# First product of tiles 3 to 8 by seven block products for pairs of tiles, weights streamed from DRAM, in an attention and feed-forward kernel

## The chip, the cores and the metric

The kernel runs on one core of one Trainium2 chip. The metric is the device time of one execution in microseconds: lower is better. TensorE (PE) multiplies, VectorE (DVE), ScalarE (ACT) and GpSimd (POOL) do the elementwise work, and SyncE (SP) issues the DMAs.

## The reference

Windowed attention over 8 batches x 8 heads x 576 positions x 64, then a feed-forward layer with a PReLU between its two products, all in float32:

```python
scores = scale * np.matmul(q, k.transpose(0, 1, 3, 2))
mask_plain = (rel >= 0) & (rel < 32)
mask_dil = (rel >= 0) & (rel < 32 * 4) & (rel % 4 == 0)
...
attn = softmax(where(mask, scores, -1e9))        # heads 0-3 plain, 4-7 dilated
x = (attn @ v).transpose(0, 2, 1, 3).reshape(8 * 576, 512)
h = x @ w_in                                     # 4608 x 512 x 2048
g = np.maximum(h, 0.0) + alpha * np.minimum(h, 0.0)
return g @ w_out                                 # 4608 x 2048 x 512
```

## The kernel before, in words

The 4608 tokens are cut into 9 tiles of 512 (`NTILE`, `TT`), the 2048 hidden columns into 16 slices of 128 (`NF`), the 512 model columns into 4 of 128 (`NC`). Everything is held transposed, so tokens are the free dimension. To keep float32 precision, every operand of the large products is held as a rounded high part and a remaining low part, and a product is three passes (high x high, high x low, low x high: `PASSES`). The weights come in as the 64-bit words of the inputs, are turned into high and low (`Conversion`), and then stay in SBUF, in tags `w0_*` to `w3_*`: `w_in` high and low, `w_out` high and low, each in three spans of slices (0 to 7, 8 and 9, 10 to 15).

A slice `(t, f)` of the feed-forward layer is `ffn_h` (12 matmuls of 128x128 on 128x512: 4 column blocks x 3 passes, into one PSUM bank), then on VectorE `ffn_parts` (PReLU in two operations), on ScalarE `ffn_high` and on VectorE `ffn_low` (the high and low part of g), then `ffn_y` (12 matmuls, 4 banks that collect over all 16 slices of the tile). After the last slice of a tile `ffn_y` copies the banks out and stores them.

Attention goes by 32 pairs of heads, four to a batch (`Pair`, index 4 b + c). For a pair, `load_qk` and `load_v` fetch, `scores` are 72 small matmuls, `maxima` 12 VectorE operations, `exponentials` 10 on ScalarE, `divisions` four on VectorE, `transposes` 5 on TensorE, `copies` 2 on ScalarE, `values` 72 small matmuls; `highs` (ScalarE) and `lows` (VectorE) write x, the input of the feed-forward layer, as high and low parts. A batch has 576 tokens and a tile 512, so a tile waits for the pairs of one or two batches.

The order on TensorE, VectorE, ScalarE and SP is the order in which the program is written (`manual_schedule`); the framework adds the semaphores. First come pairs 0 to 3 alone with the conversion of weights; then a loop over `slices`: tile 0's first 8 slices (`CUT`), tile 1, tile 0's rest (its half sum waits in DRAM, `part`), then tiles 2 to 8. In the loop, iteration n issues `ffn_h` of slice n + 1, `ffn_y` of slice n - 1, and the steps of the pairs that `score_at`, `divide_at`, `turn_at` and `value_at` put there: every second slice until tile 2 begins, then every fourth. Large matmuls are at line 337 (h) and 383 (y), scores at 158, transposes at 214, values at 232.

Of the kernel before, what the change touches and what calls it, by code (L numbers as in the profile page):

```python
# [29 lines left out]
NF = DFF // P  # L30
NROOM = 3
NG = 4
# [19 lines left out]
def tile_window_attention_prelu_ffn(  # L52
# [14 lines left out]
    const = ctx.enter_context(tc.tile_pool(name="const", bufs=1))  # L67
    xp = ctx.enter_context(tc.tile_pool(name="xp", bufs=NROOM))
# [3 lines left out]
    psp = ctx.enter_context(tc.tile_pool(name="psp", bufs=4, space=PS))  # L72
    dram = ctx.enter_context(tc.tile_pool(name="dram", bufs=1, space=bass.MemoryType.DRAM))

    ctx.enter_context(tc.manual_schedule(engines={nc.tensor.engine, nc.vector.engine, nc.scalar.engine, nc.sync.engine}))

# [3 lines left out]
    al = const.tile([P, NF], F32, name="al")  # L80
    nal = const.tile([P, NF], F32, name="nal")
    pr0 = const.tile([P, NR, BK], F32, name="pr0")
# [4 lines left out]
    part = dram.tile([NC, P, TT], F32, name="part")  # L87


# [25 lines left out]

    cells = {}

    def cell(t):
        if t not in cells:
            cells[t] = xp.tile([P, NC, 2, TT], F32R, tag="x", name=f"x_{t}")  # L120
        return cells[t]

# [3 lines left out]
    class Pair:  # L126
# [36 lines left out]
        def scores(self):  # L163
            self.ps = [psp.tile([P, NG + 2, BK], F32, tag=self.banks, name=f"s_{self.id}_{e}") for e in range(2)]
# [43 lines left out]
        def transposes(self):  # L208

            self.tp = [psp.tile([P, 3 - e, P], F32, tag=self.tbanks, name=f"t_{self.id}_{e}") for e in range(2)]  # L210
# [13 lines left out]
        def values(self):  # L224

            self.po = [psp.tile([P, HB, BQ], F32, tag="a", name=f"o_{self.id}_{u}") for u in range(2)]
            for j in range(HB):
                for u in range(2):
                    for e in range(2):
                        rows = slice(u * BK, (u + 1) * BK)  # L230
                        pt = self.pt[0][rows, 2 * P + e * BQ:] if j == HB - 1 else self.pt[e][rows, j * BQ:]
                        nc.tensor.matmul(  # L232
                            self.po[u][e * D:(e + 1) * D, j, :], lhsT=self.v[rows, e, j, :], rhs=pt[:, :BQ],
                            start=True, stop=True,
                        )

        def places(self):

            base = self.b * S
            for u in range(2):  # L240
                flat = self.po[u].rearrange("d i q -> d (i q)")
                if self.plain:
                    a, end = base + u * HQ, base + (u + 1) * HQ
                    while a < end:
                        t = a // TT
                        z = min(end, (t + 1) * TT)
                        s0 = a - base - u * HQ
                        yield flat[:, s0:s0 + z - a], [
                            cell(t)[:, self.c, e, a - t * TT:z - t * TT] for e in range(2)]
                        a = z  # L250
                else:
                    src = flat.rearrange("d (r i) -> d r i", r=2)
                    a, end = base, base + S
                    while a < end:
                        t = a // TT
                        z = min(end, (t + 1) * TT)
                        i0, i1 = (a - base) // DILATION, (z - base) // DILATION
                        yield src[:, :, i0:i1], [
                            cell(t)[:, self.c, e, a - t * TT:z - t * TT]
                            .rearrange("d (i r) -> d r i", r=DILATION)[:, 2 * u:2 * u + 2] for e in range(2)]  # L260
                        a = z

        def highs(self):
            self.out = list(self.places())
            for src, (hi, lo) in self.out:
                nc.scalar.copy(out=hi, in_=src)  # L266

        def lows(self):
            for src, (hi, lo) in self.out:
                nc.vector.tensor_tensor(out=lo, in0=src, in1=hi.bitcast(F32), op=ALU.subtract)  # L270

# [3 lines left out]
    def load_weight(which, f):  # L275
# [3 lines left out]
        else:  # L279
            st = ffp.tile([P, DM, 2], U32, tag="g", name=f"ws{which}_{f}", bufs=5)  # L280
        if which == 0:
# [49 lines left out]
    def ffn_h(t, f, first=0, end=NC):  # L331
        if first == 0:
            ms[t, f] = psp.tile([P, TT], F32, tag="a", name=f"h_{t}_{f}")
        x = cell(t)
        for c in range(first, end):
            for n, (a, e) in enumerate(PASSES):
                nc.tensor.matmul(  # L337
                    ms[t, f], lhsT=weight(0, a, f)[:, c * P:(c + 1) * P], rhs=x[:, c, e, :],
                    start=(c == 0 and n == 0), stop=(c == NC - 1 and n == 2))
# [22 lines left out]
    def ffn_high(t, f):  # L362
        g = ffp.tile([P, 2, TT], F32R, tag="g", name=f"g_{t}_{f}", bufs=5)
        nc.scalar.copy(out=g[:, 0, :], in_=ms[t, f])  # L364
        gs[t, f] = g
# [5 lines left out]
    def ffn_y(t, f):  # L371
        if (t, f) in ((0, 0), (0, CUT), (t, 0)):
            ys[t] = [psp.tile([P, TT], F32, tag="y", name=f"y_{t}_{f}_{c}") for c in range(NC)]
        g = gs.pop((t, f))
        cut, rest = (t, f) == (0, CUT - 1), t == 0 and f == NF - 1
        last = cut or f == NF - 1
        if last:
            o = [ffp.tile([P, TT], F32, tag="m", name=f"ob_{t}_{f}_{c}", bufs=5) for c in range(NC)]
        for c in range(NC):
            if rest:  # L380
                nc.sync.dma_start(out=o[c], in_=part[c])
            for n, (a, e) in enumerate(PASSES):
                nc.tensor.matmul(  # L383
                    ys[t][c], lhsT=weight(1, a, f)[:, c * P:(c + 1) * P], rhs=g[:, e, :],
                    start=(f in (0, CUT if t == 0 else 0) and n == 0), stop=(last and n == 2),
                )
        if not last:
            return
        for c in range(NC):
            if rest:  # L390
                nc.vector.tensor_tensor(out=o[c], in0=ys[t][c], in1=o[c], op=ALU.add)
            elif t == NTILE - 1:

                for i, half in enumerate((slice(0, TT // 2), slice(TT // 2, TT))):
                    if i:
                        nc.vector.tensor_copy(out=o[c][:, half], in_=ys[t][c][:, half])
                    else:
                        nc.scalar.copy(out=o[c][:, half], in_=ys[t][c][:, half])
                    nc.sync.dma_start(
                        out=outT[c * P:(c + 1) * P, t * TT + i * TT // 2:t * TT + (i + 1) * TT // 2], in_=o[c][:, half])  # L400
                continue
            elif c % 2:
# [5 lines left out]


    slices = [(0, f) for f in range(CUT)] + [(1, f) for f in range(NF)] + [(0, f) for f in range(CUT, NF)]  # L410
    slices += [(t, f) for t in range(2, NTILE) for f in range(NF)]
    NS = len(slices)
    SECOND = CUT + NF
    pairs = [Pair(b, c) for b in range(B) for c in range(NC)]
    cell(1), cell(0), cell(2)

# [34 lines left out]
    for s in range(NC):  # L451
# [3 lines left out]
        if s == 0:  # L455
# [3 lines left out]
            u.exponentials(3)  # L459
            nc.vector.tensor_scalar_mul(nal, al, -1.0)  # L460
            for op in w.words():
                op()
# [49 lines left out]
    value_at = {2 * i + 1: pairs[NC + i] for i in range(NC)}  # L512
    for p in range(2 * NC, B * NC):
        if p <= 3 * NC:
            n = SECOND - 2 + 2 * (p - 2 * NC)
        else:
            n = SECOND + CUT + 2 + 4 * (p - 3 * NC - 1)
        score_at[n] = pairs[p]
        turn_at[n + 2] = pairs[p]
        value_at[n + 2 if p < 3 * NC else SECOND + CUT + 2 + 4 * (p - 3 * NC)] = pairs[p]  # L520
    divide_at = {n + 1: u for n, u in score_at.items()}
# [65 lines left out]
    for n in range(CUT, NS):  # L587
# [4 lines left out]
        if n <= SECOND - 2:  # L592
# [6 lines left out]
            for op in words[:2]:  # L599
                op()  # L600
            ffn_low(*slices[n])
            for op in words[2:]:
                op()
# [33 lines left out]
        if scored:  # L637
            scored.exponentials(5)
        for u in pairs[2 * NC:]:
            if u is pairs[2 * NC]:  # L640
# [5 lines left out]
            if due[1]:  # L646
                u.load_v()
    ffn_y(*slices[-1])


# [51 lines left out]
```

## Time and profile before

| | |
|---|---|
| Time, median of 3 runs | 926.8 us (926.36 to 928.3) |
| Profiled execution, span | 926.4 us; first to last instruction of one execution, which is nearly all of its time |
| TensorE busy | 891.9 us (96%), granted clock 0.987 on average |
| VectorE, ScalarE, GpSimd busy | 520.2, 315.7, 0.7 us |
| Moved by DMA | 67.49 MB, 73 GB/s on average |

In the profile's lines a group of instructions has its line in the program, engine and operation, then output <- inputs by the program's names, shapes and count; after the bar the busy time in us and the mean duration of one in ns; after the second bar the idle time of the engine ahead of them and what ended it. A busy TensorE says little of its rate, since matmuls overlap; the distance between starts does.

### The profile page before, as it was taken

Reading aid. Unit: us, or ns where it says so; the run is one execution under the profiler, and the core shown is the slowest. Engines: PE = TensorE matmul, PEld = TensorE weight load, DVE = VectorE, ACT = ScalarE, POOL = GpSimd, SP = SyncE. Lnnn points to the kernel's source line nnn. Section 1 sums busy time; section 2 is a strip of 40 time slices with the busy share of each in tenths; the row PEclk is TensorE's granted clock in tenths of the full one; section 3 lists DMA queues with packets and bytes.
Section 4 is the critical chain, followed back from the end, with each engine's and each line's share of the span. In section 5 each row is a group of like instructions: output and inputs, shape, how many; then the busy total and the mean of one; then the engine's idle time right before and its main releaser. Section 6 shows DMA issues by size and latency. Waiting matters only on the chain.

```text
span 926.4 us, 19989 instructions
## 1 busy us (share of the span) xinstructions
PE 891.9 (96%) x8224; PEld 734.6 (79%) x8224; DVE 520.2 (56%) x1607; ACT 315.7 (34%) x1091; POOL 0.7 (0%) x6
## 2 busy tenths in 40 slices
PE   4669999999999999999999999999999999999998
PEld 3557888888888888888888888888888888888886
DVE  6999587775564455545544555554544543344333
ACT  5776554543432223223323323332322321111111
POOL 0000000000000000000000000000000000000000
PEclk9969999999999999999999999999999999999999
DMA  9842153222331012111211112111211010001001
GB/s 334 288 138 70 47 191 112 68 77 100 136 112 37 30 39 97 53 52 52 98 52 52 53 52 98 53 52 49 66 37 51 27 46 1 1 1 46 0 1 46
DMA packets 31867, 67.49 MB, mean 73 GB/s; under 512 B 2976, under 2 KB 12320, under 8 KB 31776
## 3 DMA queue, kind: packets, MB, share of 16 engines
q1 hardware_dynamic: 31776, 66.21, 20.7%
q8 instruction: 65, 1.06, 0.4%
q14 instruction: 26, 0.21, 0.1%
HBM read 55.71 MB, written 10.49 MB: 71 GB/s over the span
## 4 chain that ended last, share of the span: by engine, by line
PE 91%; DVE 4%; ACT 2%; DMA 1%; issue 1%; SPq 1%; DVEq 0%; ACTq 0%
PE h L337 42%; PE y L383 42%; PE o L232 3%; PE s L158 2%; PE t L214 2%; DMA ws<-w_in 1%; ACT w_dt.float L194 1%; DVE w_dt.float L182 1%; DVE w_dt.float32r L324 1%; DVE x L270 1%; DMA w_dt.uint<-w_out 0%; ACT pr L194 0%; DVE wa L313 0%; DVE wa L315 0%; ACT m L345 0%
## 5 line engine op out<-in xcount | busy, mean ns | idle before, releaser
L337 PE MATMUL h<-x,w_dt.float32r 128*128 128x512 f32 x1728 | 423.2, 394 | 7.5 <-DVE nm L182 4.7
L383 PE MATMUL y<-g,w_dt.float32r 128*128 128x512 f32 x1728 | 418.9, 391 | 0.0
L337 PEld LDWEIGHTS h<-x,w_dt.float32r 128*128 128x128 f32 x1728 | 324.2, 189 | 77.5 <-DVE x L270 4.9
L383 PEld LDWEIGHTS y<-g,w_dt.float32r 128*128 128x128 f32 x1728 | 322.0, 188 | 67.1 <-ACT ob L405 0.4
L364 ACT CAST g<-m 128x512 fp32r<-128x512 f32 x144 | 89.5, 622 | 489.3 <-DVE m L359 484.8
L358 DVE TENSOR_SCALAR m<-h,al 128x512 f32<-128x512 f32 x121 | 90.8, 751 | 247.8 <-PE h L337 247.2
L369 DVE TENSOR_TENSOR g<-m,g 128x512 fp32r<-128x512 f32 x144 | 99.1, 688 | 71.0 <-ACT g L364 71.0
L194 ACT ACTIVATE pr<-pr,nm 128x64 f32<-128x64 f32 (+1 forms) x240 | 80.3, 338 | 40.4 <-DVE nm L182 40.4
L359 DVE SCALAR_TENSOR_TENSOR m<-h,m 128x512 f32<-128x512 f32 x121 | 83.7, 691 | 4.2
L182 DVE CUSTOM_DVE_ANT_0 pr<-s,mask_sb 128x64 f32<-128x64 f32 (+1 forms) x288 | 45.1, 213 | 19.5 <-PE s L158 18.7
L270 DVE TENSOR_TENSOR x<-o,x 128x288 fp32r<-128x288 f32 (+8 forms) x112 | 36.0, 385 | 18.5 <-ACT x L266 18.2
L194 ACT ACTIVATION_READ_ACCUMULATOR pr<-pr,nm 128x1 f32 (+1 forms) x240 | 45.5, 190 | 0.0
L266 ACT CAST x<-o 128x288 fp32r<-128x288 f32 (+8 forms) x112 | 30.4, 385 | 3.8 <-PE o L232 3.8
L232 PE MATMUL o<-pt,v 64*64 64x32 f32 x1728 | 30.0, 220 | 0.0
L194 ACT ACTIVATE w_dt.float<-w_dt.float,nm 128x64 f32<-128x64 f32 (+1 forms) x80 | 26.8, 339 | 7.5 <-DVE nm L182 6.9
L232 PEld LDWEIGHTS o<-pt,v 64*64 64x64 f32 x1728 | 27.4, 135 | 2.5 <-issue 0.4
L182 DVE DVE_READ_ACCUMULATOR2_ANT nm<- 128x1 f32 (+1 forms) x384 | 28.9, 75 | 0.0
L158 PEld LDWEIGHTS s<-k,q 64*32 64x32 f32 x1728 | 19.7, 105 | 8.5 <-issue 8.5
L351 DVE SCALAR_TENSOR_TENSOR m<-m,nal,h 128x512 f32<-128x512 f32 x23 | 17.1, 744 | 16.0 <-ACT h L346 15.9
L345 ACT ACTIVATE m<-h 128x512 f32<-128x512 f32 x23 | 13.7, 595 | 35.7 <-PE h L337 35.7
L158 PE MATMUL s<-k,q 64*32 64x64 f32 x1728 | 23.5, 224 | 0.0
L221 ACT COPY pt<-t 128x320 f32<-128x320 f32 x64 | 22.4, 399 | 0.8 <-PE t L214 0.7
(48 smaller groups left out, 338.9 us busy)
## 6 DMA issues: line engine op xcount, KB each, us to landing
v<-vW SPq DMA_DIRECT2D x24, 576.0 KB, 3.8
out<-ob SPq DMA_DIRECT2D x32, 256.0 KB, 2.4
k<-kT SPq DMA_DIRECT2D x24, 288.0 KB, 4.2
q<-qT SPq DMA_DIRECT2D x24, 288.0 KB, 4.4
ws<-w_in SPq DMA_DIRECT2D x11, 512.0 KB, 3.9
w_dt.float<-vW SPq DMA_DIRECT2D x8, 576.0 KB, 7.6
ws<-w_out SPq DMA_DIRECT2D x9, 512.0 KB, 3.3
w_dt.uint<-w_out SPq DMA_DIRECT2D x7, 512.0 KB, 4.2
```

The costliest lines, as they stand in the source:

```text
L158: nc.tensor.matmul(self.ps[e][col * BQ:(col + 1) * BQ, g, :], lhsT=self.q[rows, j * BQ:(j + 1) * BQ], rhs=self.k[rows, first_key(j):first_ ...
L182: nc.vector.tensor_tensor_reduce(out=self.pr[rows, r, :], in0=self.ps[e][rows, g, :], in1=mask_sb[rows, kind, :], scale=-SCALE, scalar=3.0 ...
L194: nc.scalar.activation(out=self.pr[rows, r, :], in_=self.pr[rows, r, :], func=AF.Exp, bias=self.nm[rows, r:r + 1], scale=-1.0, accum_out=s ...
L232: nc.tensor.matmul(self.po[u][e * D:(e + 1) * D, j, :], lhsT=self.v[rows, e, j, :], rhs=pt[:, :BQ], start=True, stop=True,)
L266: nc.scalar.copy(out=hi, in_=src)
L270: nc.vector.tensor_tensor(out=lo, in0=src, in1=hi.bitcast(F32), op=ALU.subtract)
L337: nc.tensor.matmul(ms[t, f], lhsT=weight(0, a, f)[:, c * P:(c + 1) * P], rhs=x[:, c, e, :], start=(c == 0 and n == 0), stop=(c == NC - 1 a ...
L358: nc.vector.tensor_scalar(out=m, in0=ps, scalar1=0.0, scalar2=al[:, f:f + 1], op0=ALU.min, op1=ALU.mult)
L359: nc.vector.scalar_tensor_tensor(out=m, in0=ps, scalar=0.0, in1=m, op0=ALU.max, op1=ALU.add)
L364: nc.scalar.copy(out=g[:, 0, :], in_=ms[t, f])
L369: nc.vector.tensor_tensor(out=g[:, 1, :], in0=ms.pop((t, f)), in1=g[:, 0, :].bitcast(F32), op=ALU.subtract)
L383: nc.tensor.matmul(ys[t][c], lhsT=weight(1, a, f)[:, c * P:(c + 1) * P], rhs=g[:, e, :], start=(f in (0, CUT if t == 0 else 0) and n == 0) ...
```

## The change

Tiles 0 to 2 are computed as before. Tiles 3 to 8 are taken in pairs (3 and 4, 5 and 6, 7 and 8). For two tiles, two halves of the model columns and two neighbouring slices of hidden columns, h is a 2 x 2 block product, and it is formed from seven block products instead of eight, each of 6 matmuls (2 column blocks x 3 passes): Strassen's scheme, in the form that shares its sums.

*Weights.* The four sums of weight blocks that the scheme needs are formed on GpSimd (`combine`, 6 operations per pair of slices, during the last 16 slices of the loop), split into high and low on ScalarE and VectorE, and written to DRAM (`split_combined`). The plain blocks and `w_out` are written to DRAM as well (`save`, 4 DMAs per slice, in slices 24 to 39 of the loop). For tiles 3 to 8 the weights come back in units of 256 KB through a ring of 10 slots (`feed` issues a fetch, `take` uses it), 88 units for each pair of tiles.

*Tokens.* The pairs of heads write x of tiles 3 to 8 as plain float32 (ScalarE one half, VectorE the other). `token_parts` forms the seven combinations of a pair of tiles, in high and low: 4 differences and 7 lows on VectorE, 7 highs on ScalarE, each on 1024 columns. For tiles 3 and 4 this lies in the last 7 iterations of the loop (`late_ops`), with scratch in the space of ring slots 0 to 3; for the others in the phase y before.

*Phases.* A pair of tiles is two groups of 8 slices; each is a phase h (`phase_h`: four `Four` objects of 42 matmuls) and a phase y (`phase_y`: four blocks of 48 matmuls; the third and fourth product of the last Four come after the first 12). In a Four, products 1, 6, 5 and 3 add up in one bank, and ScalarE takes a snapshot after each of the first three; 7 and 4 share a second bank, 2 has a third. g of a whole group is held in SBUF, in the space of slices 0 to 7 of the weights. The sums of y of the first group wait in SBUF.

*Attention.* Pairs 8 to 19 are done by slice 45 of the loop, one every second slice; pairs 20 to 31 lie in the phases y (5, 3, 4 of them in the first, second and third) by `attention_hooks`: `begin` after 6 y matmuls of step n, `middle` after step n + 4, `end` after step n + 6, the next pair from n + 5.

The core of the diff:

```diff
+    def combine(i):
...
+        for out, x, y, op in ((4, 2, 3, ALU.add), (5, 4, 0, ALU.subtract), (6, 0, 2, ALU.subtract), (7, 1, 5, ALU.subtract)):
+            nc.gpsimd.tensor_tensor(out=t[:, out], in0=t[:, x], in1=t[:, y], op=op)
+
+    def split_combined(i):
+        t = sums_at["t"][:, 4:]
+        hi, lo = (gbuf([P, 4, 2 * P], F32R, f"wc{i}_{a}") for a in range(2))
+        nc.scalar.copy(out=hi, in_=t)
+        nc.vector.tensor_tensor(out=lo, in0=t, in1=hi.bitcast(F32), op=ALU.subtract)
+        for a, w in enumerate((hi, lo)):
+            nc.sync.dma_start(out=wS[i, 3:7, :, a].rearrange("q p n -> p q n"), in_=w.bitcast(F32))
...
+        tag = ("w2_1", "w3_1", "xA1", "xA1", "g0")[n // 2]
...
+        zeroth = [high("B11", k0), low("B11", k0), high("B21", k1), low("B21", k1)]
+        first = [diff(T1, z0, k0), high("T1", T1), low("T1", T1)]
+        second = [
+            diff(T2, z1, T1), high("T2", T2), diff(T3, z1, z0), high("T3", T3), low("T2", T2), low("T3", T3),
+            diff(T4, k1, T2), high("B22", z1), high("T4", T4), low("B22", z1), low("T4", T4),
+        ]
...
+    def product(to, q, w, start, stop):
+        name = {1: "B11", 2: "B21", 3: "B22", 4: "T4", 5: "T1", 6: "T2", 7: "T3"}[q]
+        for c in range(2):
+            for n, (a, e) in enumerate(PASSES):
+                nc.tensor.matmul(
+                    to, lhsT=w[:, (2 * a + c) * P:(2 * a + c + 1) * P], rhs=part_of(name, e)[:, c * TT:(c + 1) * TT],
+                    start=start and c == 0 and n == 0, stop=stop and c == 1 and n == 2, skip_group_check=True)
...
+        def mm(self, q):
+            w = take()
...
+            to = {1: "A", 6: "A", 5: "A", 3: "A", 2: "B", 7: "C", 4: "C"}[q]
+            product(getattr(self, to), q, w, q in (1, 2, 7), True)
+            feed()
+        def snap(self, n):
+            nc.scalar.copy(out=self.s(n), in_=self.A)
+        def add(self, n):
+            src, to = {11: ("B", 1), 22: ("C", 3), 21: ("C", 2)}[n]
+            nc.vector.tensor_tensor(out=self.s(n), in0=getattr(self, src), in1=self.s(to), op=ALU.add)
+        def negative(self, n):
...
+            nc.scalar.activation(out=self.m[n], in_=self.at(n), func=AF.Relu, scale=-1.0)
+        def value(self, n):
...
+            nc.vector.scalar_tensor_tensor(
+                out=self.m[n], in0=self.m[n], scalar=bal[:, f:f + 1], in1=self.at(n), op0=ALU.mult, op1=ALU.add)
...
+    def third(u):
+        u.mm(3)
+        u.negative(12)
+        u.high(11)
+        u.high(22)
+        u.value(12)
+
+    def fourth(u):
+        u.mm(4)
+        u.add(21)
+        u.negative(21)
+        u.low(11)
+        u.value(21)
+        u.high(12)
+
+    def after_first(u):
+        u.negative(22)
+        u.value(11)
+        u.value(22)
+
+    def phase_h(t, grp):
+        last = None
+        for i in range(GP):
+            u = Four(t, grp, i)
+            u.mm(1)
+            u.snap(1)
+            if last:
+                after_first(last)
+                third(last)
+                fourth(last)
+            u.mm(7)
+            if last:
+                last.low(22)
+                last.low(12)
+            u.mm(6)
+            u.snap(2)
+            if last:
+                last.high(21)
+            u.mm(2)
+            u.add(11)
+            if last:
+                last.low(21)
+            u.mm(5)
+            u.snap(3)
+            u.negative(11)
+            u.add(22)
+            last = u
...
+        zeroth, first, second = token_parts(NSTD, [hold(0), hold(1), hold(0), hold(0)])
+        late_ops[NS - 7], late_ops[NS - 6] = zeroth[:2], zeroth[2:]
+        late_ops[NS - 5] = first
+        late_ops[NS - 3], late_ops[NS - 2], late_ops[NS - 1] = second[:4], second[4:8], second[8:]
...
+    for _ in range(NRING - 2):
+        feed()
     ffn_y(*slices[-1])
+    feed()
+    feed()
+    paired_stage()
```

More of the change, by code (lines that the diff above doesn't have):

```diff
@@ L30 @@
 NF = DFF // P
-NROOM = 3
+NSTD = 3
+NFP = NF // 2
+AHEAD = 20
+EARLY = 21
+GP = 4
+GF = 2 * GP
+NRING = 10
 NG = 4
@@ L163, in scores @@
         def scores(self):
[L164 removed]
+            self.ps = [bank(self.banks, [P, NG + 2, BK], f"s_{self.id}_{e}") for e in range(2)]
             for g in range(NG):
@@ L224, in values @@
         def values(self):
-            self.po = [psp.tile([P, HB, BQ], F32, tag="a", name=f"o_{self.id}_{u}") for u in range(2)]
+            self.po = [bank("a", [P, HB, BQ], f"o_{self.id}_{u}") for u in range(2)]
             for j in range(HB):
@@ L371, in ffn_y @@
     def ffn_y(t, f):
-        if (t, f) in ((0, 0), (0, CUT), (t, 0)):
-            ys[t] = [psp.tile([P, TT], F32, tag="y", name=f"y_{t}_{f}_{c}") for c in range(NC)]
+        first = (t, f) in ((0, 0), (0, CUT), (1, 0), (2, CUT))
+        if first:
+            ys[t] = [bank("y", [P, TT], f"y_{t}_{f}_{c}") for c in range(NC)]
         g = gs.pop((t, f))
         cut, rest = (t, f) == (0, CUT - 1), t == 0 and f == NF - 1
-        last = cut or f == NF - 1
+        last = cut or (t, f) in ((0, NF - 1), (1, NF - 1), (2, CUT - 1))
         if last:
@@ L384, in ffn_y @@
                     ys[t][c], lhsT=weight(1, a, f)[:, c * P:(c + 1) * P], rhs=g[:, e, :],
-                    start=(f in (0, CUT if t == 0 else 0) and n == 0), stop=(last and n == 2),
+                    start=(first and n == 0), stop=(last and n == 2),
                 )
@@ new lines, in tile_window_attention_prelu_ffn, with slot, feed @@
+    ring, fed, used = {}, [0], [0]
+    def slot(n):
+        n %= NRING
+        tag = ("w2_1", "w3_1", "xA1", "xA1", "g0")[n // 2]
+        if tag not in ring:
+            ring[tag] = (ffp if tag == "g0" else const).tile(
+                [P, 8 if tag == "xA1" else 4, 2 * P], F32R, tag=tag, name=f"ring_{tag}",
+                **({"bufs": 1} if tag == "g0" else {}))
+        t = ring[tag].rearrange("p (s n) w -> p s (n w)", n=2)
+        return t[:, n - 4 if tag == "xA1" else n % 2]
+    def feed():
+        if fed[0] < len(units):
+            nc.sync.dma_start(out=slot(fed[0]).bitcast(F32), in_=units[fed[0]])
+            fed[0] += 1
@@ new lines, in take, with part_of, temporary @@
+    def take():
+        used[0] += 1
+        return slot(used[0] - 1)
+    parts, stage = {}, {}
+    BLOCKS = ("B11", "T1", "T3", "T2", "B21", "B22", "T4")
+    def part_of(name, a):
+        n = 2 * BLOCKS.index(name) + a
+        tag, k = (f"w{n}_1", 0) if n < 2 else (f"w{(n - 2) // 3}_2", (n - 2) % 3)
+        if tag not in parts:
+            parts[tag] = const.tile([P, 1 if n < 2 else 3, 2 * TT], F32R, tag=tag, name=f"parts_{tag}")
+        return parts[tag][:, k]
+    def temporary(i):
+        if i not in stage:
+            stage[i] = gbuf([P, 2 * TT], F32, f"stage{i}", i)
+        return stage[i]
@@ new lines, in small, with token_parts, diff, high @@
+    def small(i):
+        return temporary(1 + i % 8 // 2)[:, i % 2 * TT:(i % 2 + 1) * TT]
+    def token_parts(t, tmp):
+        k0, k1, z0, z1 = raw(t, 0), raw(t, 1), raw(t + 1, 0), raw(t + 1, 1)
+        T1, T2, T3, T4 = tmp
+        def diff(out, x, y):
+            return lambda: nc.vector.tensor_tensor(out=out, in0=x, in1=y, op=ALU.subtract)
+        def high(name, x):
+            return lambda: nc.scalar.copy(out=part_of(name, 0), in_=x)
+        def low(name, x):
+            return lambda: nc.vector.tensor_tensor(
+                out=part_of(name, 1), in0=x, in1=part_of(name, 0).bitcast(F32), op=ALU.subtract)
+        zeroth = [high("B11", k0), low("B11", k0), high("B21", k1), low("B21", k1)]
[4 more added lines that the diff above has]
+        ]
+        return zeroth, first, second
@@ new lines, in tile_window_attention_prelu_ffn @@
+    ABANKS = [f"a{i}" for i in range(4)]
+    def third(u):
[17 more added lines that the diff above has]
+        last = None
+        for i in range(GP):
+            u = Four(t, grp, i)
[22 more added lines that the diff above has]
+            last = u
+        return last
@@ new lines, in phase_y @@
+    def phase_y(t, grp, u, hooks):
+        end = grp + 1 == NFP // GP
+        for c in range(NC):
+            ys2 = [bank("y", [P, TT], f"y_{t}_{grp}_{c}_{tt}") for tt in range(2)]
+            for j in range(GF):
+                if j % 2 == 0:
+                    w = take()
+                for tt in range(2):
+                    g = gpart(j, tt)
+                    for n, (a, e) in enumerate(PASSES):
+                        k = 2 * (j % 2) + a
+                        nc.tensor.matmul(
+                            ys2[tt], lhsT=w[:, k * P:(k + 1) * P], rhs=g[:, e],
+                            start=j == 0 and n == 0, stop=j == GF - 1 and n == 2)
+                if j % 2:
+                    feed()
+                if c == 0 and j == 1:
+                    after_first(u)
+                    third(u)
+                    fourth(u)
+                    u.low(22)
+                    u.low(12)
+                    u.high(21)
+                    u.low(21)
+                for op in hooks.get(GF * c + j, ()):
+                    op()
+            for tt in range(2):
+                if not end:
+                    if tt:
+                        nc.vector.tensor_copy(out=partial(c, tt), in_=ys2[tt])
+                    else:
+                        nc.scalar.copy(out=partial(c, tt), in_=ys2[tt])
+                    continue
+                o = ffp.tile([P, TT], F32, tag="m", name=f"ob_{t}_{c}_{tt}", bufs=5)
+                nc.vector.tensor_tensor(out=o, in0=ys2[tt], in1=partial(c, tt), op=ALU.add)
+                nc.sync.dma_start(out=outT[c * P:(c + 1) * P, (t + tt) * TT:(t + tt + 1) * TT], in_=o)
@@ new lines, in attention_hooks, with put, begin, middle @@
+    def attention_hooks(hooks, us, start, step):
+        def put(n, *ops):
+            hooks.setdefault(n, []).extend(ops)
+        for k, u in enumerate(us):
+            n = start + step * k
+            nxt = pairs.index(u) + 1
+            def begin(u=u, nxt=nxt):
+                u.scores()
+                if nxt < len(pairs):
+                    pairs[nxt].load_qk()
+                u.maxima()
+                u.exponentials()
+            def middle(u=u):
+                u.divisions()
+                u.transposes()
+                u.copies()
+            def end(u=u, nxt=nxt):
+                u.values()
+                if nxt < len(pairs):
+                    pairs[nxt].load_v()
+                u.highs()
+                u.lows()
+            put(n, begin)
+            put(n + step - 1, middle)
+            put(n + step + 1, end)
@@ new lines, in paired_stage @@
+    def paired_stage():
+        todo = pairs[AHEAD:]
+        for u in todo:
+            u.banks = u.tbanks = "a"
+        for t in range(NSTD, NTILE, 2):
+            for grp in range(NFP // GP):
+                hooks = {}
+                last = phase_h(t, grp)
+                if t == NSTD:
+                    us, todo = (todo[:5], todo[5:]) if grp == 0 else (todo[:3], todo[3:])
+                else:
+                    us, todo = (todo[:4], todo[4:]) if grp == 0 else ([], todo)
+                attention_hooks(hooks, us, 2, 5)
+                if grp and t + 2 < NTILE:
+                    lots = token_parts(t + 2, [temporary(i) for i in range(1, 5)])
+                    for at, lot in zip((4, 10, 20) if t == NSTD else (4, 10, 16), lots):
+                        for k, op in enumerate(lot):
+                            hooks.setdefault(at + k, []).append(op)
+                phase_y(t, grp, last, hooks)
@@ L460, in tile_window_attention_prelu_ffn @@
             nc.vector.tensor_scalar_mul(nal, al, -1.0)
+            nc.vector.tensor_scalar(out=bal, in0=al, scalar1=-1.0, scalar2=1.0, op0=ALU.mult, op1=ALU.add)
             for op in w.words():
@@ L601, in tile_window_attention_prelu_ffn @@
             ffn_low(*slices[n])
+            if divided and n < SECOND - 2:
+                divided.divisions()
             for op in words[2:]:
```

190 lines of the change are left out of this document (149 added, 41 removed).

## The prediction

> **What bounds the kernel now.** I read the page's busy table first, then busy time by stretch, then the groups of instructions, the chain that ended last, and the timeline around one attention pair.
>
> ```profile
> span 926.4 us, 19989 instructions
> ...
> PE 891.9 (96%) x8224; PEld 734.6 (79%) x8224; DVE 520.2 (56%) x1607; ACT 315.7 (34%) x1091; POOL 0.7 (0%) x6
> ...
> DMA packets 31867, 67.49 MB, mean 73 GB/s; under 512 B 2976, under 2 KB 12320, under 8 KB 31776
> ...
> L337 PE MATMUL h<-x,w_dt.float32r 128*128 128x512 f32 x1728 | 423.2, 394 | 7.5 <-DVE nm L182 4.7
> L383 PE MATMUL y<-g,w_dt.float32r 128*128 128x512 f32 x1728 | 418.9, 391 | 0.0
> ...
> out<-ob SPq DMA_DIRECT2D x32, 256.0 KB, 2.4
> k<-kT SPq DMA_DIRECT2D x24, 288.0 KB, 4.2
> ```
>
> Busy time by stretch (stretch and its length, then each engine's busy us, the granted clock, the DMA engines' share, GB/s):
>
> ```profile
> 10.00:15.00 5.00, 3.26 (x107) 2.47 (x96) 3.42 (x20) 1.13 (x5) 0.00 (x0) 1.00 1.05 394
> 45.00:50.00 5.00, 0.27 (x2) 0.00 (x0) 3.80 (x9) 5.00 (x19) 0.00 (x0) 0.55 0.61 196
> 50.00:55.00 5.00, 4.34 (x141) 3.88 (x144) 5.00 (x12) 3.20 (x7) 0.00 (x0) 0.50 0.05 17
> 200.00:300.00 100.00, 100.00 (x1259) 82.36 (x1258) 58.63 (x235) 38.38 (x166) 0.00 (x0) 1.00 0.28 97
> 742.14:913.73 171.59, 171.59 (x757) 142.09 (x758) 69.95 (x101) 22.45 (x39) 0.00 (x0) 1.00 0.04 13
> ```
>
> The chain (start us, length us, what):
>
> ```profile
> 58.64 4.81 PE h L337 x12
> 215.40 2.76 PE y L383 x12
> 229.20 2.76 PE y L383 x12
> 272.71 2.96 PE h L337 x12
> 278.39 2.72 PE h L337 x12
> 303.08 2.72 PE h L337 x12
> 913.73 8.17 PE y L383 x36
> ```
>
> From 100 us to the end TensorE never rests; 3456 large matmuls set the time. One takes 8.17/36 = 0.227 us (mean "391" overlaps the next), so twelve take 2.72 us and a slice (h and y) 5.45. From 278.39 to 303.08 lie four slices and one pair: 24.69 - 21.79 = 2.9 us of TensorE per attention pair, small matmuls and switching together. Pairs at every second slice also run without a hole (215.40 to 229.20 is 13.80 = 10.89 + 2.9). So removed matmuls come off the time in full, unless something new makes TensorE wait. The profiled span agrees with the median of the runs (926.8) within 0.05%, so I sum against 926.4 and correct nothing.
>
> **The change, part by part.**
>
> *Fewer matmuls.* Per two tiles and 256 hidden columns, eight block products of six matmuls become seven. Three pairs of tiles x 8 such column pairs x 6 = 144 fewer: -144 x 0.227 = **-32.7 us**. The y matmuls are as many as before.
>
> *Phase h: can the other engines follow?* A Four is 42 matmuls, 9.53 us; a product is 1.36 us.
>
> ```profile
> L364 ACT CAST g<-m 128x512 fp32r<-128x512 f32 x144 | 89.5, 622 | 489.3 <-DVE m L359 484.8 <-DVE m L351 3.3 <-DVE rs L201 0.8
> L369 DVE TENSOR_TENSOR g<-m,g 128x512 fp32r<-128x512 f32 x144 | 99.1, 688 | 71.0 <-ACT g L364 71.0
> L351 DVE SCALAR_TENSOR_TENSOR m<-m,nal,h 128x512 f32<-128x512 f32 x23 | 17.1, 744 | 16.0 <-ACT h L346 15.9
> L405 ACT COPY ob<-y 128x512 f32<-128x512 f32 x16 | 8.8, 598 | 2.1 <-DMA part<-ob 2.1
> L398 ACT COPY ob<-y 128x256 f32<-128x256 f32 x4 | 1.5, 372 | 4.9 <-PE y L383 4.9
> L403 DVE COPY ob<-y 128x512 f32<-128x512 f32 x16 | 10.3, 683 | 3.4 <-DMA part<-ob 3.4
> L396 DVE COPY ob<-y 128x256 f32<-128x256 f32 x4 | 1.7, 424 | 4.4 <-ACT ob L398 4.4
> masks.py:199 POOL TENSOR_SCALAR_AFFINE_SELECT ident<-ident 128x128 f32<-128x128 f32 x1 | 0.3, 294 | 0.1
> ```
>
> ScalarE gets 3 snapshots, 4 negatives, 4 highs: 11 x 0.61 = 6.7 us. VectorE gets 3 additions, 4 values, 4 lows: 11 x 0.71 = 7.8 us. Both are under 9.53, but TensorE adds on to the bank that a snapshot reads, so order counts.
>
> ```profile
> 278.23 2.89 PE L337 MATMUL h<-x,w_dt.float32r 128*128 128x512 f32 x12
> 281.15 0.75 DVE L358 TENSOR_SCALAR m<-h,al 128x512 f32<-128x512 f32 x1 [2.11 <-PE h L337]
> ```
>
> A reader starts 281.15 - 278.23 - 2.72 = 0.2 us after the last matmul's slot. Count from the end of a Four's product 5. Snapshot 3 runs 0.2 to 0.8; product 3 adds to that bank at 1.36, after the next Four's product 1: 0.5 us spare. Snapshot 2 starts 0.2 after product 6 and is done at 0.8, and product 5 comes 1.36 after product 6: again 0.5 spare, if ScalarE is free. It is: its queue before that (high of 12) ends 0.5 us before product 6 does. Product 4's bank is read by the addition for 22, done at 1.6, wanted at 2.72; product 2's by that for 21, done at 5.0, wanted at 6.8. So I take **0**. Bounds: 0, and one ScalarE operation late twice in each of 24 Fours, 2 x (0.6 - 0.5) x 24 = 5 us; a longer queue is a rival below.
>
> *The stream.* 3 x 88 = 264 units of 256 KB are fetched. In phase h one per 1.36 us, 193 GB/s (10:15 above moved 394); in phase y one per 2.72. The slot is asked for again nine products before use: 12 us.
>
> ```profile
> 397.10 0.52 SPq L146 DMA_DIRECT2D k<-kT  x1
> ```
>
> An issue takes SP some 0.5 us, and landing 2.4 to 4.2 (stores and k loads on the page): **0**, hidden by the ring. Past SP's queue also go the k, q, v loads (behind scores and values, which TensorE has just done) and the outputs (behind VectorE's add): each holds the feeds for about a microsecond of the 12.
>
> *Tiles 0 to 2.* Pairs 8 to 19 now come every second slice: as at 215 to 229, no hole; TensorE's part only moves. Added from slice 32: a split per two slices. A 1024-wide VectorE operation is extrapolated from 424 and 683 ns to 1.2 us, ScalarE's from 372 and 598 to 1.05. VectorE goes from 58.6% (200:300 above) by 1.2/13.8 to some 67%: hidden. POOL's sums (two of 512, four of 256 columns) at 294 ns per 128 columns take 4.7 us of 13.8; between VectorE's own prices (2 x 0.683 + 4 x 0.424 = 3.1) and twice POOL's, 9.4. The saves, splits and loads are 0.92 + 0.52 + 0.59 MB per 6.9 us, 294 GB/s: under 394, **0**. But half of the saves go in runs of 512 bytes, which I can't price from a row: between the same rate, and half of it, where the queue would fall behind some 0.3 us a slice, 2.5 us in all, inside the 13 us by which loads are early. The Trainium skill (DMA: Bandwidth & Descriptors, Specifications) gives 512 bytes as the least for line rate; by it, too, this term is 0.
>
> *The hand-over to the paired stage.* Here the cover ends. Count from the start of the last h group. TensorE has h, then y of slices 45, 46, 47: 4 x 2.72 = 10.9, and 0.6 for the last g. VectorE enters late: the lows of pair 19, behind its values, end at 1.0 (an estimate), then, in queue order, split (after ScalarE) to 3.4, two differences to 5.8, the parts of slice 47 with its low to 8.8 (ScalarE between), two lows and a difference to 12.4, split 13.6, lows of B22 and T4 16.0. The first ring slot is T4's scratch, so its fetch waits for 16.0; I take 3.5 us for landing (between 2.4 and 4.2, behind 1 MB of split writes): 19.5 - 11.5 = **8.0 us** idle. Bounds: 4 (VectorE's queue runs unbroken at its rate) and 13 (POOL's last sum at 9.4 us, slow landing). Then the clock: after the idle at 45:50 it stands at 0.55 and then 0.50, and the group at 58.64 took 4.81 rather than 2.72: **+2.1**.
>
> *Attention inside phase y.*
>
> ```profile
> 295.24 0.98 PE L158 MATMUL s<-k,q 64*32 64x64 f32 x72
> 296.53 0.35 ACT L194 ACTIVATE pr<-pr,nm 128x64 f32<-128x64 f32 x1 [1.72 <-DVE nm L182]
> 274.13 0.35 ACT L194 ACTIVATE pr<-pr,nm 128x64 f32<-128x64 f32 x1
> 275.47 0.34 ACT L194 ACTIVATE pr<-pr,nm 64x64 f32<-64x64 f32 x1
> 277.10 0.16 DVE L201 TENSOR_SCALAR rs<-sums 128x10 f32<-128x10 f32 x1
> 277.55 0.89 DVE L204 TENSOR_TENSOR pr<-pr,rs 128x512 f32<-128x512 f32 x2
> ```
>
> From the start of the scores: first exponential 1.3 later, ten at (275.47 - 274.13)/4 = 0.335, divisions 1.34 (277.10 to 278.44): transposes can start 6.1 us after. TensorE meanwhile has scores, four groups of six (5.45), and the previous pair's values: 7.7 or more. No wait, except for the first pair of a phase: its maxima queue behind the last Four's low of 21, which ends 4.5 us after product 4; then 0.3 + 3.35 + 1.34 puts the transposes at 9.5, and TensorE gets there at 8.0: 1.5 us, in two phases. In the third (tiles 3 and 4, second half) B11's high and low are queued ahead of the divisions, 1.05 + 1.2 more: 3.9 us. Together **6.9**, and a half-chance of a clock dip after the last, **+1.0**. Values no longer follow scores directly, so there is a third switch per pair at 2.96 - 2.72 = 0.24: 12 x 0.24 = **2.9**. Bounds: 3 (switching only) and 20 (every pair waits 1.5 us).
>
> *The token parts* of later pairs: 11 VectorE and 7 ScalarE operations of 1024 in a 44 us phase y; T4 is done before the last groups: hidden.
>
> *The end.*
>
> ```profile
> 913.56 8.32 PE L383 MATMUL y<-g,w_dt.float32r 128*128 128x512 f32 x36
> 920.32 3.76 SPq L399 DMA_DIRECT2D out<-ob  x8
> ```
>
> The last matmul's slot ends at 913.56 + 8.17 = 921.7, so 4.7 us follow, held by SP issuing eight stores. Afterwards: two VectorE adds (ends at 0.9), an issue of 0.5, 2.4 to land: 3.9, **-0.8**.
>
> Smaller edits (fixed bank tags, `bal`, raw copies in place of high and low for tiles 3 to 8, partial sums kept in SBUF: 8 copies of 0.6 a phase, split over two engines): **0**, behind matmuls.
>
> Sum: 926.4 - 32.7 + 8.0 + 2.1 + 6.9 + 1.0 + 2.9 - 0.8 = 913.8, so **914 us**.
>
> **The rivals.**
>
> 1. *Slower: the snapshot chain in phase h doesn't keep its 0.5 us.* Snapshots 2 and 3 sit in a strict queue with highs that wait for VectorE. If that queue runs one and a half operations late, each of 24 Fours loses 1 us: 914 + 24 = 938. It decides from 0.53 us per Four (12.6/24). For it: ScalarE above sat 484.8 us behind VectorE's results. Against: both are well under 9.53 us. Chance 0.19.
> 2. *The ring starves.* Were fetches to reach only 140 GB/s, a unit takes 1.87 us and each of six phases h loses 14 us: 1000. Against: 394 GB/s above. Chance 0.04.
> 3. *POOL holds VectorE.* No row has POOL at work beside VectorE. If VectorE's operations with both inputs in SBUF wait while POOL's last sum runs, 4.7 us go on to the hand-over: 919. The Trainium skill (SBUF — State Buffer, Who interferes with whom) says just that: such an instruction and a GpSimd one that reads SBUF lock each other out. Chance 0.12.
> 4. *The hand-over is nearly covered* (idle 4, little clock loss, few attention waits): 914 - 4 - 2 - 5 = 903. Chance 0.13.
> 5. *The matmuls gain nothing*, because products of six with a wait each run slower than 0.227: at 0.235 the 1008 lose 8 us, 922. Chance 0.07.
>
> **How the numbers follow.** The forecast case (906 to 922) has 0.45. From no change, this kernel tells 0.2%, about 1.9 us. Faster than 924.9: 0.43 + 0.12 + 0.13 + 0.05 = 0.73, less 0.02 for mishaps that add up; rivals 1 and 2 are slower but for 0.02, with some of 5: 0.22; between, 0.07. The range leaves out 1 in 10 below (under 902) and 1 in 10 above (over 934, the worse half of rival 1 and rival 2); the forecast case alone is 906 to 922.
>
> **What will show it.** 3312 matmuls of 512 columns; some 160 MB moved (67.5 + 23 written + 69 fetched). A TensorE hole of about 8 us near 366 us, ended by a fetch, VectorE busy through it, then a group near 4.8 us. Six phases h of 38 us with TensorE at 100%, SP waiting for TensorE and not the reverse. If TensorE waits for ScalarE's snapshot in every Four, rival 1 holds; if for fetches, rival 2. Forty-two matmuls in more than 9.6 us without a named wait are rival 5. In phase y the only waits should stand before transposes.

## The result, and the profile after

The changed kernel takes 933.2 us (930.2 to 935.7) against 927.1 for the kernel before: ratio 1.0066 (95% interval 1.0044 to 1.0089), and once more, in the first set of experiments, 1.0081 (1.0068 to 1.0095). It is some 0.7% slower; 914 us, faster, was forecast. The profiled execution took 930.15 us, with a span of 928.4: 1.75 us lie around the span, and it is the fastest of the four, while spans of others were up to 934.0. One execution further below, the profiled one of the kernel with eight products, ran in a slow state (3120 us), so the median there is of the other three and the table of losses leaves that kernel out.

The page of the changed kernel: span, busy times, DMA.

```profile
span 928.4 us, 20670 instructions
...
PE 871.6 (94%) x8080; PEld 710.5 (77%) x8080; DVE 554.2 (60%) x1607; ACT 426.0 (46%) x1250; POOL 55.7 (6%) x54
...
DMA packets 101314, 159.83 MB, mean 172 GB/s; under 512 B 8416, under 2 KB 47456, under 8 KB 101216
```

TensorE has 144 instructions less (8224 to 8080) and 20 us less of busy time, and yet the span is 2 us longer. So TensorE now waits, which it did not after the first 100 us. For whom, says the view of waits (engine and line, what it waited for: us, times, longest); the lines named `w_dt.float` or `nm` are of the first 100 us and are not new, so I leave them out, with four others of at most 1.5 us each:

```profile
PE t L248 <- DVE pr L238: 13.7, 14, 3.7
...
PE pA L561 <- DMA ring_w<-wS: 6.9, 1, 6.9
...
PE y L422 <- DVE ob L430: 1.8, 1, 1.8
...
PE s L192 <- DVE m L397: 0.8, 1, 0.8
```

Transposes wait for the divisions (line 238) 14 times, the ring once, at the hand-over. Cut to the paired stage, the same view has only two lines:

```profile
PE t L248 <- DVE pr L238: 7.2, 6, 3.1
PE pA L561 <- DMA ring_w<-wS: 6.9, 1, 6.9
```

Half of the waits for divisions thus lie in the loop, where I had put down nothing. The chain shows the phases themselves (start, length, what):

```profile
385.51 2.90 PE pA L561 x6
...
392.60 4.08 PE pA L561 x18
...
402.12 4.08 PE pA L561 x18
...
411.63 4.08 PE pA L561 x18
...
802.23 40.80 PE y L699 x180
```

A Four takes 402.12 - 392.60 = 9.52 us, 42 x 0.2267, and 180 y matmuls in a row take 40.80: both phases run at TensorE's own rate. The first product after the hand-over takes 2.90 rather than 1.36; the granted clock stands at 0.66 between 385 and 390 us. The hand-over itself, in the timeline:

```profile
381.53 1.22 DVE L546 TENSOR_TENSOR parts_w<-hold,parts_w 128x1024 fp32r<-128x1024 f32 x1
...
382.78 1.76 SPq L508 DMA_DIRECT2D ring_w<-wS  x4
```

The low part of T4 is VectorE's last use of the scratch; it ends at 382.75, the first fetch into that space leaves at 382.78, and TensorE starts 2.7 us later, at 385.51.

To see where the time stays I took, from the starts of the values (line 266) of successive pairs, the time between them less 0.2269 per large matmul and 2.9 per pair. In the kernel before, this is nothing (within 0.5 us) for every pair from pair 8 on, but for -0.9 at the last. The sums of it, in us; the columns are the changed kernel's profile of above and the kernels of the next section, in their order (without the one of eight products, see above), and the second row takes in the first pair of the phases:

| | changed | again | no_sums | odd_sums | ring | later | early_saves | all | writes | no_sums_t1 |
|---|---|---|---|---|---|---|---|---|---|---|
| loop, slices 23 to 45 (pairs 8 to 19) | 13.7 | 14.5 | 7.7 | 6.3 | 14.6 | 15.4 | 12.2 | 3.7 | 9.5 | 8.6 |
| hand-over (pairs 19 to 20) | 11.2 | 11.8 | 11.3 | 10.2 | 11.1 | 10.4 | 11.5 | 3.5 | 11.0 | 11.3 |
| phases y (pairs 20 to 31) | 10.3 | 10.2 | 10.2 | 10.3 | 10.0 | 2.9 | 10.3 | 1.6 | 10.2 | 10.2 |

And this is the worst place of the loop, in the timeline of the changed kernel (start, length, engine, line; the wait in brackets):

```profile
353.50 4.75 POOL L468 TENSOR_TENSOR wsum<-wsum 128x256 f32<-128x256 f32 x4 [6.94 <-DVE wc L474]
...
355.61 1.38 DVE L546 TENSOR_TENSOR parts_w<-hold,parts_w 128x1024 fp32r<-128x1024 f32 x1 [1.12 <-ACT parts_w L543]
...
358.33 2.94 POOL L465 TENSOR_TENSOR wsum<-w_dt.float32r 128x512 f32<-128x512 f32 x2
...
358.74 2.67 DVE L238 TENSOR_TENSOR pr<-pr,rs 128x512 f32<-128x512 f32 x2
360.26 0.20 PEld L248 LDWEIGHTS t<-ident,pr 128*128 128x128 f32 x2 [4.13 <-issue]
360.29 0.41 PE L248 MATMUL t<-ident,pr 128*128 128x128 f32 x2 [3.74 <-DVE pr L238]
```

The two divisions that took 0.89 us before (277.55) take 2.67, and end just as POOL's two wide sums end, at 361.3; TensorE stands for 3.74 us before the transposes, and 0.86 more before the last three of them. Not all of this is POOL's: the split (line 474) and T1's operations (lines 540 to 546) stand ahead of the divisions in VectorE's queue, and without POOL's sums (next section) a wait of 2.76 us remains here. The wait costs more than itself: from 361 to 366 us the granted clock is 0.66, and the twelve matmuls of y that follow take 4.14 us, where other groups of twelve take 2.9.

### The profile page after: what moved, and what is told of

Same layout as the page of the kernel before. It is cut to its first block, busy times and chain, and to the rows that moved or that the text cites. A ratio compares the mean times of both kernels' runs of the same rounds, so it can differ in the third digit from the quotient of the medians.

```text
span 928.4 us, 20670 instructions
## 1 busy us (share of the span) xinstructions
PE 871.6 (94%) x8080; PEld 710.5 (77%) x8080; DVE 554.2 (60%) x1607; ACT 426.0 (46%) x1250; POOL 55.7 (6%) x54
## 3 DMA queue, kind: packets, MB, share of 16 engines
q8 instruction: 64, 1.05, 0.5%
## 4 chain that ended last, share of the span: by engine, by line
PE 54%; DVE 3%; ACT 2%; DMA 0%; issue 0%; ACTq 0%
PE y L699 26%; PE pA L561 14%; PE pC L561 7%; PE pB L561 4%; PE o L266 2%; ACT pr L228 1%; PE t L248 1%; PE s L192 1%; DVE gp L629 1%; DVE n L621 0%; DVE pr L238 0%; ACT n L617 0%; DMA ring_w<-wS 0%; DVE ob L722 0%; DVE stage L610 0%
## 5 line engine op out<-in xcount | busy, mean ns | idle before, releaser
L375 PE MATMUL h<-x,w_dt.float32r 128*128 128x512 f32 x576 | 145.6, 403 | 6.1 <-DVE nm L216 5.2
L422 PE MATMUL y<-g,w_dt.float32r 128*128 128x512 f32 x576 | 141.3, 395 | 1.8 <-DVE ob L430 1.8
L375 PEld LDWEIGHTS h<-x,w_dt.float32r 128*128 128x128 f32 x576 | 109.9, 194 | 30.5 <-issue 5.9
L422 PEld LDWEIGHTS y<-g,w_dt.float32r 128*128 128x128 f32 x576 | 107.6, 189 | 25.0 <-DVE ob L430 2.1
L699 PE MATMUL y<-gp,ring_w 128*128 128x512 f32 x480 | 114.7, 393 | 0.0
L699 PE MATMUL y<-gp,ring_xA 128*128 128x512 f32 x444 | 107.9, 396 | 0.0
L699 PEld LDWEIGHTS y<-gp,ring_w 128*128 128x128 f32 x480 | 89.0, 188 | 18.6
L699 PEld LDWEIGHTS y<-gp,ring_xA 128*128 128x128 f32 x444 | 83.1, 190 | 17.4
L402 ACT CAST g<-m 128x512 fp32r<-128x512 f32 x48 | 29.8, 621 | 84.9 <-DVE m L397 80.6
L629 DVE TENSOR_TENSOR gp<-n,gp 128x512 fp32r<-128x512 f32 x96 | 63.1, 684 | 0.0
```

The source lines that it names most:

```text
L375: nc.tensor.matmul(ms[t, f], lhsT=weight(0, a, f)[:, c * P:(c + 1) * P], rhs=half(t, c)[:, e, :], start=(c == 0 and n == 0), stop=(c == NC ...
L422: nc.tensor.matmul(ys[t][c], lhsT=weight(1, a, f)[:, c * P:(c + 1) * P], rhs=g[:, e, :], start=(first and n == 0), stop=(last and n == 2),)
L629: nc.vector.tensor_tensor(out=g[:, 1], in0=self.m.pop(n), in1=g[:, 0].bitcast(F32), op=ALU.subtract)
L699: nc.tensor.matmul(ys2[tt], lhsT=w[:, k * P:(k + 1) * P], rhs=g[:, e], start=j == 0 and n == 0, stop=j == GF - 1 and n == 2)
```

## The experiments

Numbers in the table above. Unless said, a kernel differs from the changed one by its edit alone.

**The changed kernel again.** 

> The changed kernel once more, unaltered, as the measure for the others of this set. Both theories: 930 to 936 us, 0.3 to 0.9% over the kernel before; divisions (128x512 and 64x128) at a mean near 0.87 us in slices with POOL's sums, and TensorE some 14 us behind between 190 and 366 us.

934.5 us, ratio 1.0081 (1.0068 to 1.0095). The measure for what follows.

**Without POOL's sums.**

```diff
         if "t" not in sums_at:
             sums_at["t"] = const.tile([P, 8, 2 * P], F32, tag="xA1", name="wsum")
+            nc.gpsimd.memset(sums_at["t"], 0.5)
+        return
```

> Leaves out POOL's 48 sums (the buffer is filled once instead, so the weights of four products are constants). Theory (POOL's sums hold VectorE's operations that read two SBUF operands, the divisions above all, and TensorE's transposes wait for these): divisions back at a mean of 0.49 us, the loss of 14 us before 366 us falls to 3 to 6, the time falls by 8 to 11 us, to about 924. Rival (VectorE's and ScalarE's queues are simply too full with splits and token parts): these are all still there, so the time falls by less than 2 us.

926.2 us, 0.9998 (0.9981 to 1.0015): 8.3 us less. VectorE's groups between 275 and 350 us, first of the changed kernel, then of this one:

```profile
L238 DVE TENSOR_TENSOR pr<-pr,rs 128x512 f32<-128x512 f32 (+1 forms) x10 | 8.3, 870 | 0.2
L397 DVE SCALAR_TENSOR_TENSOR m<-h,m 128x512 f32<-128x512 f32 x10 | 6.9, 692 | 0.3
L235 DVE TENSOR_SCALAR rs<-sums 128x10 f32<-128x10 f32 x5 | 1.9, 372 | 0.0
```

```profile
L238 DVE TENSOR_TENSOR pr<-pr,rs 128x512 f32<-128x512 f32 (+1 forms) x10 | 4.4, 485 | 0.2
L235 DVE TENSOR_SCALAR rs<-sums 128x10 f32<-128x10 f32 x5 | 0.8, 162 | 0.0
```

The divisions go from a mean of 870 ns to 485; the operation that reads PSUM and one SBUF operand (line 397) has 692 beside POOL, as the kernel before had 691. The split, the token parts and the saves are all still there, so the rival (full queues) holds for the other 7.7 us of the loop at most.

**The sums in the odd slices.**

```diff
-        if n >= SECOND + CUT:
-            k = n - SECOND - CUT
+        if SECOND + CUT - 1 <= n < NS - 1:
+            k = n - SECOND - CUT + 1
```

> Sums and splits one slice earlier: the split ends an even slice, so POOL's six sums run in the odd slice, where maxima and PReLU (one SBUF operand) are VectorE's work, and not in the even one with the divisions. Theory: of the 14 us some 6 to 9 go, and the hand-over gets 1 to 2 us shorter: 922 to 927 us, divisions near 0.5 us. Rival (full queues, or DMA writes): the work is the same and only moved, so 931 to 935.

924.5 us, 0.9971 (0.9961 to 0.9982): 10.0 us less than the changed kernel, and faster than the kernel before. The work is the same; the divisions are back:

```profile
L238 DVE TENSOR_TENSOR pr<-pr,rs 128x512 f32<-128x512 f32 (+1 forms) x10 | 4.4, 484 | 0.2
```

This is also 1.7 us under the kernel without sums. The likely reason is that the split no longer stands ahead of the divisions: the transposes of the last pair in the loop, which wait for 2.76 us without sums, wait for under 0.3 here, and the hand-over loses 10.2 us, not 11.3. The split was not moved alone.

**Eight products.**

```diff
             product(getattr(self, to), q, w, q in (1, 2, 7), True)
+            if q == 4:
+                product(getattr(self, to), q, w, False, True)
```

> Product 4 of every Four is multiplied twice (its value counts double), so that a Four has eight products, 48 matmuls. Theory (TensorE alone sets the pace of phase h, so a product more or less counts in full): 24 x 6 x 0.227 = 32.7 us more than the changed kernel, about 965. Rival (ScalarE and VectorE set the pace of phase h): under 25 us more.

965.1 us, ratio 1.0417 (1.0401 to 1.0433) against 1.0081: about 31 us more, of 32.7, and the difference of two such ratios is good to some 2 us. So the removed matmuls count in full, or nearly; the scheme does what it says, and everything built around it costs some 39 us.

**Another order of the ring.**

```diff
-        tag = ("w2_1", "w3_1", "xA1", "xA1", "g0")[n // 2]
+        tag = ("xA1", "xA1", "w3_1", "w2_1", "g0")[n // 2]
...
-        return t[:, n - 4 if tag == "xA1" else n % 2]
+        return t[:, n if tag == "xA1" else n % 2]
```

> The ring's first four slots are now those in POOL's buffer and the last two those in T4's scratch; nothing else is altered. Theory (the hole at the hand-over is the wait for T4's scratch and then a landing): the hole of 7.0 us shrinks to 2 to 4, and with a shorter clock loss the time is 4 to 6 us under the changed kernel, 928 to 931. Rival (the hole is the landing itself, or the fetches queue behind the split writes): under 1.5 us gained.

932.6 us, 1.0060 (1.0044 to 1.0076): 0.6 to 2 us less than the changed kernel, against its two ratios (1.0066 and 1.0081); that is hardly more than the intervals, and not 4 to 6. The timeline:

```profile
372.04 11.87 SPq L476 DMA_DIRECT2D wS<-wc  x4
...
382.30 1.22 DVE L474 TENSOR_TENSOR wc<-wsum,wc 128x1024 fp32r<-128x1024 f32 x1
...
384.00 2.48 SPq L508 DMA_DIRECT2D ring_xA<-wS  x4
...
387.57 2.90 PE L561 MATMUL pA<-parts_w,ring_xA 128*128 128x512 f32 x6 [5.88 <-DMA ring_xA<-wS]
```

The hole is 5.9 us instead of 6.9. The first fetch no longer waits for T4's scratch, in use till 385.8 here. It leaves at 384.0, directly behind the last write of the split on SP's queue (372.04 + 11.87 = 383.9); that write, and POOL's buffer into which the fetch now goes, both wait for the last split, which ends at 383.5. So the rival's queue behind the split writes and the release of the buffer come at nearly the same moment, and this run can't part them. Taking one of two late releases away shows the other.

**Transposes one step later.**

```diff
-            put(n + step - 1, middle)
-            put(n + step + 1, end)
+            put(n + step, middle)
+            put(n + step + 2, end)
```

> In the phases y the divisions and transposes of a pair come one step of six matmuls later, and so do its values. Theory (TensorE waits 0.7 to 3.3 us before transposes, 8 us in all, because the divisions are late by about that): most of these waits go, and transposes stand directly before the next scores, one switch less: 5 to 8 us under the changed kernel, 926 to 930. Rival (the chain from scores to divisions is set by banks or by the order behind the values, and moves along): under 2 us.

925.4 us, 0.9982 (0.9973 to 0.9991): 8 to 9 us less. The phases' loss falls from 10.3 to 2.9, of which 1.8 is one wait behind B11's parts.

**Earlier saves.**

```diff
-        if SECOND <= n < SECOND + NF:
-            save(n - SECOND)
+        if SECOND - 9 <= n < SECOND - 9 + NF:
+            save(n - SECOND + 9)
```

> The plain weights are written to DRAM in slices 15 to 30 and not 24 to 39. Theory (of the 14 us about 2 are the half sums of tile 0 that come late from DRAM behind the saves on SP's queue and on the DMA engines; the rest is POOL): 2 to 3 us under the changed kernel, 930 to 933, and y of slice 32 waits under 0.5 us for its output buffers. Rival (DMA writes are what slows slices 32 to 39): 6 us or more.

931.0 us, 1.0045 (1.0031 to 1.0060): 2 to 3.5 us less; the wait for line 430 falls from 1.8 us to 0.2. The rest of the loop's loss stays, so the saves are not its cause. The split's own writes were not moved here.

**All in one.** The four edits, and `(7, 12, 20)` in place of `(4, 10, 20)` for the first token parts in a phase y.

> The earlier sums, the new order of the ring, the later transposes and the earlier saves in one, and B11's and B21's parts three steps later in the phase y that has three pairs. Theory (the losses lie in different places and add up): 10 from the sums, 5, 6 and 2: some 22 us under the changed kernel, 910 to 915, under the kernel before by 1.2 to 1.8%. Rival (they hide one another): 918 or more.

907.6 us, ratio 0.9792 (0.9775 to 0.9808): the losses add up, and more, since the ring's order now pays: the split is done a slice earlier, and the hand-over loses 3.5 us, where the ring alone left 11.1 and the earlier sums alone 10.2. The fifth edit was not run alone; beside the later transposes the phases' loss goes from 2.9 to 1.6. Its waits, of those listed above:

```profile
PE pA L561 <- DMA ring_xA<-wS: 1.4, 1, 1.4
...
PE t L248 <- DVE pr L238: 0.7, 2, 0.5
```

**POOL writes only.** Six fills, `nc.gpsimd.memset(t[:, 4:], 0.5)`, in place of the six sums.

> POOL's six sums are replaced by six fills of 1024 columns in the same place (the weights of four products are constants then): POOL is busy at the same times, but only writes. Theory (what holds VectorE is POOL's reading of SBUF beside VectorE's second operand): divisions at a mean of 0.5 us beside a busy POOL, and a time as without sums, 924 to 928. Rival (any POOL work on SBUF holds VectorE): divisions over 0.7 us, 931 to 935.

929.4 us, 1.0022 (1.0004 to 1.0039), between the two. Groups of this kernel, VectorE's between 275 and 350 us:

```profile
L464 POOL MEMSET wsum<- 128x1024 f32 x48 | 45.8, 954 | 328.3 <-PE h L375 248.7 <-DVE wc L470 77.2
```

```profile
L238 DVE TENSOR_TENSOR pr<-pr,rs 128x512 f32<-128x512 f32 (+1 forms) x10 | 4.4, 485 | 0.2
L235 DVE TENSOR_SCALAR rs<-sums 128x10 f32<-128x10 f32 x5 | 3.6, 723 | 0.0
L236 DVE RECIPROCAL rs<-rs 128x10 f32<-128x10 f32 x5 | 1.1, 217 | 0.2
```

The divisions, with two SBUF inputs, are free of a POOL that writes; the tiny addition of 10 columns (line 235), with one SBUF input and an SBUF output, isn't: 723 ns instead of 162. The reciprocal behind it (line 236), of the same size and also from SBUF to SBUF, keeps its 217. The addition stands ahead of the divisions, so part of the loss comes back by another door. The expectation was right on the divisions and short on the time.

**T1 a slice later, without sums.** `late_ops[NS - 4] = first`.

> Without POOL's sums, and with the first three token parts that are formed from two tiles (T1) one slice later, in the even slice 44 and not behind the split of slice 43. Theory (the 2.9 us for which transposes still waited without sums came from T1's operations queued ahead of the divisions): that wait goes, 2 to 4 us under the kernel without sums, 922 to 924. Rival (the divisions are late there from the split alone): no change, 926.

927.4 us, 0.9996 (0.9984 to 1.0007): nothing gained. The wait of 2.8 us before the transposes is gone, and in its place stands one before the values (first in the list of waits, then in the timeline):

```profile
PE o L266 <- ACT pt L255: 2.9, 2, 2.6
```

```profile
359.55 1.22 DVE L548 TENSOR_TENSOR parts_w<-hold,parts_w 128x1024 fp32r<-128x1024 f32 x1 [1.11 <-ACT parts_w L545]
360.69 0.74 DVE L396 TENSOR_SCALAR m<-h,al 128x512 f32<-128x512 f32 x1
...
362.27 0.62 ACT L402 CAST g<-m 128x512 fp32r<-128x512 f32 x1 [2.75 <-DVE m L397]
362.79 0.69 ACT L255 COPY pt<-t 128x320 f32<-128x320 f32 x2
...
363.26 1.52 PE L266 MATMUL o<-pt,v 64*64 64x32 f32 x72 [2.58 <-ACT pt L255]
364.71 4.61 PE L375 MATMUL h<-x,w_dt.float32r 128*128 128x512 f32 x12
```

T1's three operations run one after the other between VectorE and ScalarE; moved behind the divisions, they delay the PReLU of slice 45, its rounding on ScalarE waits for that, and the copies of the transposes queue behind the rounding. The group of twelve after it takes 4.61 us, at a granted clock of 0.66 between 364 and 369 us, where it took 3.02 in the kernel without sums. So the first half of the theory is shown and the gain is not.

## Why the prediction was wrong, point by point

- *Fewer matmuls, -32.7:* right (about 31 by the kernel with eight products, within some 2 us).
- *The range:* 933.2 us lies just inside the 902 to 934 that I gave, by luck: its upper part was there for rival 1, which did not happen.
- *Phase h, 0, and the stream, 0:* right. A Four takes 9.52 us of 9.53 forecast, and the ring is waited for once, at its start. Rivals 1, 2 and 5 are out.
- *Tiles 0 to 2, 0:* the step that failed. It cost 13.7 us and turns the sign: 913.8 + 13.7 = 927.5, against a span of 928.4. I compared busy shares (67% of VectorE) and priced POOL's sums against their 13.8 us period only. What I named as POOL's effect (rival 3) I placed at the hand-over alone, at 4.7 us, with a chance of 0.12. But the four narrow sums of a combination (from the second on) are released by the split before it, at the end of an odd slice; the two wide sums of the next combination follow at once, and together they run into the divisions of the even slice. Removing the sums took 6.8 us out of the loop (14.5 to 7.7), moving them and the splits by a slice 8.2. The rest of the 13.7: some 2 us for tile 0's half sums, late behind the saves, on SP's queue or on the DMA engines (shown by the earlier saves, which don't part the two), T1's operations and the split ahead of the divisions, some 3 us (pairs 18 and 19 without sums; the odd slices take most of it away), and 1.1 us of scores that wait for a bank (line 397), in every changed kernel, whose cause I did not try.
- *POOL's price:* 4.7 us a combination, bounds 3.1 to 9.4; measured 4 x 0.98 + 2 x 1.55 = 7.0, and 4 x 0.82 + 2 x 1.38 = 6.0 in the odd slices: the waiting goes both ways.
- *Hand-over, 8.0 + 2.1:* a wait of 6.9, and 2.90 - 1.36 = 1.5 for the first product: near, and by the path that I named: T4's scratch came free 15.4 us after the start of the last h group (16.0 in the forecast), and the landing took 2.7 (3.5). But a second release, the last split, whose writes end on SP at 380.9, lay only 1.9 us ahead of it, and I didn't see it.
- *Attention in phases y, 6.9 + 1.0 + 2.9:* 7.2 us of named waits (1.05 of them in the table's row of the hand-over) and 10.3 by the table, whose switches lie in the 2.9 only as far as before. The total is near, in part by luck: the three first pairs wait for 1.05, 3.1 and 1.04 us, 5.2 in all where I put 6.9, and three later pairs, for which I put no wait, for 0.6 to 0.7 each.
- *The end:* the last y matmul's slot ends at 924.5, 3.9 us before the end, as forecast.
- *The measure:* I took span and median as one. By the runs here some 1.75 us lie around a span, so the profiled execution of before was probably one of its slower ones; and the changed kernel's executions spread over 5.6 us. Of the 19 us missed, 933.2 - 928.4 = 4.8 are of this kind; the loop is nearly all of the rest.
- *Small slips in the working:* the sum for the end gives 3.8 and not 3.9, and that for the transposes 6.0 and not 6.1. The 0.3 us a slice for saves at half the rate doesn't come out of my figures: 0.46 MB at half of 394 GB/s and the rest at the whole take 6.3 us of a slice's 6.9. None of these moves the forecast.

## What to carry to other kernels

A share of busy time says whether an engine has room, not whether it has room when a chain needs it: for each added stream ask what releases it, and lay it beside the operations that are late at that moment. Idle GpSimd is not free for VectorE; put its sums beside work that reads PSUM, and away from short operations on a chain that TensorE waits for. When several small waits remain, take them away together: each alone (10, 8 to 9, 2 to 3.5 and at most 2 us) looked modest, and all together, with one more, some 25 to 27.

## What the runs showed of the hardware

Two rules in one: POOL reading SBUF stretched VectorE's operations with two SBUF inputs (485 to 870 ns on average, 0.89 to 2.67 us for one pair), POOL writing did not (485), and operations with a PSUM input did not care (692). The Trainium skill (SBUF — State Buffer, Who interferes with whom) says so, and these traces agree. I had not expected that an operation with a single SBUF input, of 10 columns, would wait for POOL's fills (162 to 723 ns); the same section has it for operations that enter a mode with two ports, and no run here shows the mode itself. It is not every operation with one SBUF input: the reciprocal of the same size kept 217 ns beside the fills. And a wait of TensorE can cost more than its length: after the one of 3.74 us before the transposes the granted clock was 0.66 for some 5 us, and twelve matmuls took 4.14 us, where 2.9 is usual. The length of the wait alone doesn't decide it in these runs: after 2.76 us without sums the clock stayed at 1.00, and after 2.58 us in the last kernel it fell to 0.66.
